# A new issue order for one turn of a block-causal attention with a mixture-of-experts tail, on one Trainium2 core: values copied at once, one PSUM bank fewer

## The chip, the core and the metric

The kernel runs on one core of one Trainium2 chip. The core has five engines that work on their own queues and meet at semaphores: TensorE (PE, matmuls and transposes; PEld is its weight load), VectorE (DVE), ScalarE (ACT), GpSimd (POOL) and SyncE (SP, which here only issues DMAs). The metric is the device time of one execution in microseconds, lower is better. The time of a kernel is the median of several executions; before and after are compared on the same chip.

## What is computed

The reference, cut to what matters (batch 8, 8 heads, 576 positions, 64 per head; 4608 tokens, 8 experts of 512 to 1024 to 512, at most 80 tokens each):

```
scores = (q @ k.T) / sqrt(64);  scores[block_i < block_j] = -1e9     # blocks of 64 positions
attn   = exp(scores - max);  attn /= sum + 1e-9;  x = attn @ v       # per batch and head
logits = x @ w_gate;  e = argmax(logits);  gate = softmax(logits)[e] # x as 4608 x 512
for each expert: of its tokens keep the `capacity` with the largest gate
    out[token] = gate * (relu(x[token] @ w1[e]) @ w2[e]);  every other row is 0
```

## The kernel before, in words

The attention works on **pairs**: two heads of one batch, 32 pairs in all, four to a batch. Head 0 lies on partitions 0 to 63 and head 1 on 64 to 127. A pair's 576 query positions are five row groups: 0 to 3 of 128 rows, and 4 of 64 rows (both heads side by side in one tile).

A pair goes through these steps. The names are the methods of `Pair` and stand in the tables that the change edits:

- `load`, `load_v`: DMAs on SP's queue. `load` issues four DMAs for q and then four for k, into a buffer pair that two pairs share by turns; so the load for pair i+2 has to wait until pair i's tiles have been transposed.
- `prep 0` and `prep 1`: DVE transposes q (0) or k (1) to T0 or T1 (line 405). POOL then scales T0 (line 408).
- `scores g`: PE computes one PSUM tile of scores (pool `ps_s`, two tiles of two banks): "3", "20" (row groups 2 and 0 together), "1", and `scores_4`. Lines 423, 430 and 439.
- `max g`, `max_4`: DVE takes the negated row maximum from PSUM (lines 444 and 448).
- `soft u h`, `soft_4`: ACT computes the exponential from PSUM into SBUF and sums the rows (lines 452 and 457).
- `back x`: PE transposes blocks of the exponentials into a PSUM tile (line 485): "30" and "31" (row group 3, head 0 or 1), "20", "2", "1", each four blocks; "4" four blocks; "44" one block.
- `take back x`: DVE ("v") or ACT ("a"), by the table `TAKE`, copies that tile to PT in SBUF (lines 519 and 517).
- `values 0` and `values 1`: PE multiplies by v into a PSUM tile (line 505): 512 positions, and the last 64. `take values` copies them to xT on ACT (line 517).
- `flip`: DVE turns xT into Y for the store (line 273).

PSUM has eight banks. `ps_s` takes four; the other four belong to the pool `ps_m`, from which every `back` tile, both `values` tiles and the tiles of the deferred steps below are drawn. A new `ps_m` tile is put in a bank whose last tile has been read out in the order of the program; if that reading is not done when PE gets there, PE waits.

The issue order is written out by hand: the table `TURN` is gone through once per turn, and each entry names a pair relative to the turn's own (0 is this turn's pair, -1 the one before, and so on). Each engine gets its instructions in this order, and the schedule is not touched after that. So `scores`, `max` and `soft` of pair i share a turn with `back 4`, `back 44` and `values` of pair i-1.

When a batch's four pairs are through, nine deferred steps are queued, and the three entries `(0, "step")` of each of the next three turns take one each: turn A does `recip` (DVE), `store` (SP) and `logits 0` (PE, ACT, line 290); turn B does `logits 1`, `logits2 0` and `logits2 1` (PE transposes the logits, line 302, DVE multiplies them, line 308); turn C does `gate` (DVE), `turn` (POOL) and `turn2` (PE, line 356, and DVE, line 360). The fourth turn has no deferred step; it is called plain here. A, B and C come up for seven of the eight batches; the last batch's steps follow the loop, and so does the expert part (lines 814 and on), which both versions share.

Of the kernel before, what the change touches and what calls it, by code (L numbers as in the profile page):

```python
# [7 lines left out]
F32 = mybir.dt.float32  # L8
# [10 lines left out]
P = 128  # L19
# [5 lines left out]
CHUNK = 80  # L25


TAKE = {"back": {"30": "v", "31": "a", "1": "a", "2": "a", "20": "v", "4": "v", "44": "v"}, "values": {0: "a", 1: "a"}}

GROUPS = {"3": ((3, 0),), "20": ((2, 0), (0, 384)), "1": ((1, 0),)}  # L30

# [3 lines left out]
    (0, "begin"),  # L35
    (0, "scores", "3"),
    (0, "scores", "20"),
    (-1, "back", "4"),
    (-1, "back", "44"),
    (0, "max", "3"),  # L40
    (-1, "take", "back", "4"),
    (-1, "take", "back", "44"),
    (0, "max", "20"),
    (0, "soft", 3, 0),
    (0, "soft", 3, 1),
    (-1, "values", 0),
    (0, "soft", 0, 0),
    (0, "soft", 0, 1),
    (-1, "values", 1),
    (0, "step"),  # L50
    (1, "prep", 0),
    (0, "soft", 2, 0),
    (0, "soft", 2, 1),
    (0, "scores", "1"),
    (0, "max", "1"),
    (0, "back", "30"),
    (0, "back", "31"),
    (0, "step"),
    (0, "scores_4"),
    (1, "prep", 1),  # L60
    (-1, "take", "values", 0),
    (0, "take", "back", "31"),
    (0, "take", "back", "30"),
    (0, "soft", 1, 0),
    (0, "soft", 1, 1),
    (0, "max_4"),
    (0, "back", "20"),
    (0, "back", "2"),
    (0, "soft_4"),
    (0, "take", "back", "20"),  # L70
    (0, "take", "back", "2"),
    (-1, "take", "values", 1),
    (0, "step"),
    (0, "back", "1"),
    (0, "take", "back", "1"),
    (-2, "flip"),
)


# [1 line left out]
def tile_attn_moe(ctx, tc, q, k, v, w_gate, w1, w2, capacity, out, xs=None, dbg=None):  # L81
# [170 lines left out]
    ps_m = attp.enter_context(tc.tile_pool(name="ps_m", bufs=4, space=PSUM))  # L252

    class Batch:
        def __init__(self, b):
            self.b = b
            self.xT = big.tile([P, NP, S], F32, name="xT")
            self.Y = big.tile([P, S // 32, NP, 32], F32, name="Y")
            self.sums = sm.tile([P, NT, H], F32, name="sums", bufs=2)
            self.sums4 = sm.tile([P, NP], F32, name="sums4", bufs=2)  # L260
            nc.gpsimd.memset(self.sums[BLK:P, NT - 1, :], 1.0)
            self.rs = sm.tile([P, NT, H], F32, name="rs", bufs=2)
# [110 lines left out]
    class Pair:  # L373


        def __init__(self, i):
            self.i = i
            self.b, self.pr = divmod(i, NP)
            self.h0 = 2 * self.pr
            self.out = {}  # L380
            self.T = []

        def load(self):

# [17 lines left out]
        def prep(self, x):  # L402

            t = qk.tile([P, S], F32, name=f"T{x}")
            nc.vector.transpose(t, self.nat[x].rearrange("p g d -> p (g d)"))  # L405
            self.T.append(t)
            if x == 0:
                nc.gpsimd.tensor_scalar(t, t, scalar1=SCALE, scalar2=1.0, op0=ALU.mult, op1=ALU.mult)  # L408

# [51 lines left out]
        def back(self, x):  # L461


            if x == "30":
                self.PT = big.tile([P, 2, 13, P], F32, name="PT")
            PT = self.PT
            row = Pt[self.i % 2]
            pt = ps_m.tile([P, 512], F32, name="pm")
            if x in ("30", "31"):
                h = int(x[1])  # L470
                blocks = [(3, h, j) for j in range(4)]
                dst = PT[:, h, 3:13:3]
            elif x in ("1", "2"):
                u = int(x)
                blocks = [(u, h, j) for h in range(2) for j in range(2)]
                dst = PT[:, :, u:u + 4:3]
            elif x == "20":
                blocks = [b for h in range(2) for b in ((0, h, 0), (2, h, 2))]
                dst = PT[:, :, 0:9:8]
            else:  # L480
                blocks = [(4, None, j) for j in (range(4) if x == "4" else (4,))]
                dst = PT[:, :, 10:12] if x == "4" else PT[:, 0, 7]
            for n_, (u, h, j) in enumerate(blocks):
                src = row[u] if h is None else row[u][:, h]
                nc.tensor.transpose(pt[:, P * n_:P * (n_ + 1)], src[:, P * j:P * (j + 1)], ident)  # L485
            src = pt[:, 0:P * len(blocks)]
            if len(dst.shape) == 3:
                src = src.rearrange("p (j c) -> p j c", c=P)
            elif len(dst.shape) == 4:
                src = src.rearrange("p (h j c) -> p h j c", h=2, c=P)  # L490
            self.out["back", x] = (dst, src)

        def values(self, half):

            av = ps_m.tile([P, 512], F32, name="pm")
            PT = self.PT
            for j in range(4 + half):
                for h in range(2):
                    lhs = self.vt[:, h, :] if j == 4 else self.vn[:, h, j, :]
                    if half == 0:  # L500
                        rhs, c0, end = PT[:, h].rearrange("p b c -> p (b c)")[:, 512 * j:512 + 384 * j], P * j, 512
                    else:
                        b = PT[:, 0, 7] if j == 4 else PT[:, j // 2, 10 + j % 2]
                        rhs, c0, end = b[:, h * BLK:(h + 1) * BLK], 0, BLK
                    nc.tensor.matmul(av[h * D:(h + 1) * D, c0:end], lhsT=lhs, rhs=rhs,  # L505
                                     start=(j == 0), stop=(j == 3 + half))
            self.out["values", half] = ((self.bt.xT[:, self.pr, 0:512], av) if half == 0 else
                                        (self.bt.xT[:, self.pr, 512:S], av[:, 0:BLK]))
# [5 lines left out]
        def take(self, what, x):  # L514

            if TAKE[what][x] == "a":
                nc.scalar.copy(*self.out.pop((what, x)))  # L517
# [71 lines left out]
    ps_m = ctx.enter_context(tc.tile_pool(name="ps_m2", bufs=3, **ps))  # L589
# [292 lines left out]
    with tc.For_i(0, again, 1):  # L882
# [24 lines left out]
        step = 1.0  # L907
# [161 lines left out]
```

## Time and profile before

| | |
|---|---|
| median of 3 runs | 500.9 us (500.85 to 501.71) |
| the profiled execution's own time | 499.57 us |
| its span, from first to last instruction | 497.5 us |
| PE busy with matmuls | 445.1 us, 89% of the span |
| DVE, ACT, POOL busy | 311.7, 253.9, 52.5 us |
| mean granted TensorE clock | 0.976 of full speed |
| attention loop (first scores of the first pair to those of the last) | 7.9 to 347.6 us |

The profile shows one execution. Its time is 2.1 us above its span, and 1.3 us below the median of the runs. A row of the timeline gives the start, the busy time, the engine, the source line and the tiles (out<-in); in square brackets stands how long the engine was idle before and what ended that. Rows of merged instructions carry their count. A matmul's row ends at a modelled time, so PE's pace is best read from the starts of weight loads.

### The profile page before, as it was taken

What the parts mean: (1) busy time and instruction counts of PE and PEld (TensorE: products, weight loads), DVE (VectorE), ACT (ScalarE), POOL (GpSimd) and SP (SyncE); (2) the same over time, 40 slices, a digit from 0 to 9 for tenths busy, and PEclk for the clock granted to TensorE, in tenths of its full rate; (3) what the DMA queues carried; (4) which work ended last, traced back from release to release, by engine and by line L of the source; (5) the groups of instructions that cost most, each with busy time, mean ns of one, the idle gap of its engine ahead of it and who ended that gap; (6) DMA issues with size and microseconds to landing.
All of it is one profiled execution on the core that took longest, in us unless ns stands there. A gap on an engine that the chain in (4) does not pass through costs nothing. (4 is left out here: it accounts for less than half of the span.)

```text
span 497.5 us, 13600 instructions
## 1 busy us (share of the span) xinstructions
PE 445.1 (89%) x5403; PEld 308.3 (62%) x5403; DVE 311.7 (63%) x628; ACT 253.9 (51%) x799; POOL 52.5 (11%) x111
## 2 busy tenths in 40 slices
PE   5999999899899989999998999999985788889991
PEld 3666656556556556655665565556554677778991
DVE  5678787888688878869787886878673220110110
ACT  2677577667666656766765677667612110111100
POOL 1110201010010001001000101010012600000010
PEclk9899999999999999999999999999998599999997
DMA  5776457358647875686679888899596699993010
GB/s 93 134 128 120 79 107 139 67 91 157 104 76 156 176 179 117 126 190 143 129 162 275 180 262 153 177 261 181 132 380 192 190 355 397 398 390 115 17 30 20
DMA packets 232982, 84.32 MB, mean 169 GB/s; under 512 B 196877, under 2 KB 215309, under 8 KB 232912
## 3 DMA queue, kind: packets, MB, share of 16 engines
q1 hardware_dynamic: 231888, 80.93, 66.6%
q0 software_dynamic: 1024, 2.43, 1.7%
q8 instruction: 46, 0.75, 0.7%
q14 instruction: 24, 0.20, 0.1%
HBM read 63.21 MB, written 20.33 MB: 168 GB/s over the span
## 5 line engine op out<-in xcount | busy, mean ns | idle before, releaser
L452 ACT ACTIVATE P<-sc,negm 128x512 f32<-128x512 f32 (+3 forms) x256 | 132.7, 528 | 90.2 <-DVE negm L444 84.2
L444 DVE TENSOR_REDUCE negm<-sc 128x2 f32<-128x1024 f32 (+3 forms) x128 | 101.9, 817 | 46.6 <-PE sc L430 46.4
L485 PE MATMUL pm<-ident,P 128*128 128x128 f32 x800 | 112.8, 281 | 10.6 <-DVE prod L308 5.9
L485 PEld LDWEIGHTS pm<-ident,P 128*128 128x128 f32 x800 | 85.7, 141 | 44.0 <-issue 26.1
L423 PE MATMUL sc<-T,T 64*128 64x128 f32 (+3 forms) x512 | 89.9, 466 | 3.0 <-ACT P L452 1.8
L505 PE MATMUL pm<-PT,vn 128*64 128x64 f32 (+4 forms) x1024 | 91.1, 330 | 0.5 <-DVE PT L519 0.3
L519 DVE COPY PT<-pm 128x512 f32<-128x512 f32 (+1 forms) x128 | 71.0, 575 | 11.1 <-PE pm L485 11.1
L505 PEld LDWEIGHTS pm<-PT,vn 128*64 128x64 f32 x1024 | 52.1, 137 | 40.5 <-issue 34.9
L423 PEld LDWEIGHTS sc<-T,T 64*128 64x128 f32 x512 | 41.6, 186 | 31.4 <-issue 7.1
L517 ACT COPY PT<-pm 128x512 f32<-128x512 f32 x96 | 56.4, 589 | 2.4 <-PE pm L485 0.3
L408 POOL TENSOR_SCALAR T<-T 128x576 f32<-128x576 f32 x32 | 21.5, 671 | 307.0 <-PE pm L505 140.3
L452 ACT ACTIVATION_READ_ACCUMULATOR P<-sc,negm 128x1 f32 x256 | 52.1, 204 | 0.0
L405 DVE STREAM_TRANSPOSE T<-ld 128x576 f32<-128x576 f32 x64 | 48.8, 763 | 3.7 <-DMA ld<-in_k_dram 2.0
L814 PE MATMUL ps<-xsT,w 128*64 128x80 f32 x1024 | 41.6, 242 | 5.4 <-issue 5.4
L814 PEld LDWEIGHTS ps<-xsT,w 128*64 128x64 f32 x1024 | 39.3, 144 | 5.7 <-issue 5.1
L814 PE MATMUL av<-hT,w 128*64 128x80 f32 x1024 | 38.3, 234 | 4.4 <-issue 4.4
L814 PEld LDWEIGHTS av<-hT,w 128*64 128x64 f32 x1024 | 36.5, 137 | 6.3 <-issue 6.3
L439 PE MATMUL sc<-T,T 64*64 64x288 f32 x256 | 39.0, 424 | 0.7 <-ACT P L452 0.7
L457 ACT ACTIVATE P<-sc,negm 128x576 f32<-128x576 f32 x32 | 23.7, 740 | 24.9 <-DVE negm L448 24.9
L834 ACT ACTIVATE hT<-ps 128x320 f32<-128x320 f32 x16 | 7.0, 437 | 50.2 <-PE ps L814 50.2
L842 DVE COPY yT<-av 128x320 f32<-128x320 f32 x8 | 3.9, 492 | 37.2 <-PE av L814 37.2
L448 DVE TENSOR_REDUCE negm<-sc 128x1 f32<-128x576 f32 x32 | 24.0, 751 | 5.0 <-PE sc L439 4.9
(158 smaller groups left out, 304.1 us busy)
## 6 DMA issues: line engine op xcount, KB each, us to landing
w<-in_moe_w_dram SPq DMA_DIRECT2D x16, 2048.0 KB, 16.7
ld<-in_q_dram SPq DMA_DIRECT2D x128, 72.0 KB, 2.7
ld<-in_k_dram SPq DMA_DIRECT2D x128, 72.0 KB, 2.7
xs<-Y SPq DMA_DIRECT2D x32, 288.0 KB, 5.3
out_dram<-zero SPq DMA_DIRECT2D x18, 512.0 KB, 3.5
vn<-in_v_dram SPq DMA_DIRECT2D x64, 128.0 KB, 2.8
vt<-in_v_dram SPq DMA_DIRECT2D x32, 32.0 KB, 2.5
xs<-rs SPq DMA_DIRECT2D x8, 16.0 KB, 4.3
```

The costliest lines, as they stand in the source:

```text
L405: nc.vector.transpose(t, self.nat[x].rearrange("p g d -> p (g d)"))
L423: nc.tensor.matmul(s[:, h, c:c + P * (u + 1)], lhsT=self.T[0][r, P * u:P * (u + 1)], rhs=self.T[1][r, 0:P * (u + 1)], start=(x == 0), stop ...
L439: nc.tensor.matmul(s[r, c, 0:288], lhsT=self.T[0][r, 512:S], rhs=self.T[1][r, 288 * c:288 * (c + 1)], start=True, stop=True)
L444: nc.vector.tensor_reduce(self.negm[:, u], self.s[g][:, :, c:c + P * (u + 1)], axis=AX.X, op=ALU.max, negate=True)
L448: nc.vector.tensor_reduce(self.negm[:, 4, 0:1], self.s["4"][:, :, 0:288], axis=AX.XY, op=ALU.max, negate=True)
L452: nc.scalar.activation(Pt[self.i % 2][u][:, h], self.s[g][:, h, c:c + P * (u + 1)], AF.Exp, bias=self.negm[:, u, h:h + 1], scale=1.0, accu ...
L457: nc.scalar.activation(Pt[self.i % 2][4][:, 0:S].rearrange("p (c k) -> p c k", c=2), self.s["4"][:, :, 0:288], AF.Exp, bias=self.negm[:, 4 ...
L485: nc.tensor.transpose(pt[:, P * n_:P * (n_ + 1)], src[:, P * j:P * (j + 1)], ident)
L505: nc.tensor.matmul(av[h * D:(h + 1) * D, c0:end], lhsT=lhs, rhs=rhs, start=(j == 0), stop=(j == 3 + half))
L517: nc.scalar.copy(*self.out.pop((what, x)))
L519: nc.vector.tensor_copy(*self.out.pop((what, x)))
L814: yield nc.tensor.matmul(dst(b)[64 * c:64 * (c + 1)], lhsT=w_[:, a, col:col + 64], rhs=x_[:, a], start=(a == 0), stop=(a == n - 1))
```

## The change

It edits the table `TURN` and four other lines. On DVE, k is transposed before q, early in the turn, and the copy of `back 20` and that of `back 44` move to ACT. On ACT, both copies of the values stand together behind the exponentials of row groups 3, 2 and 0. `values 1` no longer draws a tile from `ps_m` but uses columns 128 to 191 of the tile of `back 44`. Since k is now transposed first, q and k are kept by name (`self.T[x]`) and not in the order of arrival. The second and third deferred step of a turn stand at other places: behind `scores 1`, and behind `scores_4`.

```
-TAKE = {"back": {... "20": "v", "4": "v", "44": "v"}, ...}
+TAKE = {"back": {... "20": "a", "4": "v", "44": "a"}, ...}
 TURN = (
...
-    (0, "step"),
-    (1, "prep", 0),
+    (-1, "values", 1),
+    (1, "prep", 1),
...
-            self.T = []
+            self.T = {}
...
-            self.T.append(t)
+            self.T[x] = t
...
             self.out["back", x] = (dst, src)
+            if x == "44":
+                self.shared = pt
...
-            av = ps_m.tile([P, 512], F32, name="pm")
+            av = ps_m.tile([P, 512], F32, name="pm") if half == 0 else self.shared[:, P:2 * P]
```

Behind the change the source lines from 493 on stand two lines further down in the changed file (519 is 521 there, 517 is 519).

The order of DVE in one plain turn, before: row maxima (`negm`), copies of "4" (2x256) and "44" (128), T0 from q, T1 from k, copies of "30" and "20", the flip (Y). The number behind a name tells tiles apart.

```order
L444 TENSOR_REDUCE negm_809<-sc_810 128x2
L519 COPY PT_733<-pm_822 128x2x256
L519 COPY PT_733<-pm_827 128x128
L444 TENSOR_REDUCE negm_809<-sc_815 128x2 x2
L405 STREAM_TRANSPOSE T0_858<-ld0_653 128x576
L444 TENSOR_REDUCE negm_809<-sc_863 128x2
L405 STREAM_TRANSPOSE T1_885<-ld1_654 128x576
L519 COPY PT_869<-pm_870 128x4x128
L448 TENSOR_REDUCE negm_809<-sc_880 128x1
L519 COPY PT_869<-pm_893 128x2x2x128
L273 STREAM_TRANSPOSE Y_214<-xT_213 128x18x32
```

The same turn of DVE in the changed kernel:

```order
L444 TENSOR_REDUCE negm_805<-sc_806 128x2
L444 TENSOR_REDUCE negm_805<-sc_811 128x2 x2
L521 COPY PT_732<-pm_821 128x2x256
L405 STREAM_TRANSPOSE T1_853<-ld1_651 128x576
L444 TENSOR_REDUCE negm_805<-sc_859 128x2
L405 STREAM_TRANSPOSE T0_878<-ld0_650 128x576
L521 COPY PT_867<-pm_868 128x4x128
L448 TENSOR_REDUCE negm_805<-sc_882 128x1
L273 STREAM_TRANSPOSE Y_214<-xT_213 128x18x32
```

T1 (k) has moved ahead of the maximum of "1" and T0 (q) behind it; the copies of "44" and "20" are gone from DVE.

The order of ACT in the same turn, before: exponentials (P), then the copy of `values 0` (xT, 512), of "31", and near the end that of `values 1` (xT, 64) between the copies of "2" and "1".

```order
L452 ACTIVATE P1_3_131,sums_670<-sc_810,negm_809 128x512 x2
L452 ACTIVATE P1_0_128,sums_670<-sc_815,negm_809 128x128 x2
L452 ACTIVATE P1_2_130,sums_670<-sc_815,negm_809 128x384 x2
L517 COPY xT_668<-pm_836 128x512
L517 COPY PT_869<-pm_875 128x4x128
L452 ACTIVATE P1_1_129,sums_670<-sc_863,negm_809 128x256 x2
L457 ACTIVATE P1_4_132,sums4_671<-sc_880,negm_809 128x576
L517 COPY PT_869<-pm_898 128x2x2x128
L517 COPY xT_668<-pm_847 128x64
L517 COPY PT_869<-pm_907 128x2x2x128
```

And in the changed kernel:

```order
L519 COPY PT_732<-pm_819 128x128
L452 ACTIVATE P1_3_131,sums_667<-sc_806,negm_805 128x512 x2
L452 ACTIVATE P1_2_130,sums_667<-sc_811,negm_805 128x384 x2
L452 ACTIVATE P1_0_128,sums_667<-sc_811,negm_805 128x128 x2
L519 COPY xT_665<-pm_819 128x64
L519 COPY xT_665<-pm_830 128x512
L452 ACTIVATE P1_1_129,sums_667<-sc_859,negm_805 128x256 x2
L519 COPY PT_867<-pm_873 128x4x128
L457 ACTIVATE P1_4_132,sums4_668<-sc_882,negm_805 128x576
L519 COPY PT_867<-pm_900 128x2x2x128
L519 COPY PT_867<-pm_888 128x2x2x128
L519 COPY PT_867<-pm_893 128x2x2x128
```

The copy of `values 1` has moved from the end of the turn to its middle, and reads the tile (pm_819) that the copy of "44" has read; three copies of transposes now end the turn.

PE's order in a turn B, before, from `logits 1` on: line 302 are the transposes of the logits, line 485 those of the exponentials.

```order
L290 MATMUL pm_1113<-xT_213,wgd_99 32x192 x4
L423 MATMUL sc_1124<-T1_1014,T0_981 128x256 x2
...
L485 MATMUL pm_1131<-ident_79,P1_3_131 128x128 x4
L485 MATMUL pm_1136<-ident_79,P1_3_131 128x128 x4
L302 MATMUL pm_1141<-ident_79,lgT_1036 128x128 x4
L439 MATMUL sc_1148<-T1_1014,T0_981 64x288 x4
...
L485 MATMUL pm_1166<-ident_79,P1_2_130 128x128 x4
L302 MATMUL pm_1175<-ident_79,lgT_1036 64x128
L485 MATMUL pm_1179<-ident_79,P1_1_129 128x128 x4
```

In the changed kernel:

```order
L290 MATMUL pm_1109<-xT_213,wgd_99 32x192 x4
L423 MATMUL sc_1118<-T1_971,T0_1006 128x256 x2
...
L302 MATMUL pm_1124<-ident_79,lgT_1016 128x128 x4
L485 MATMUL pm_1134<-ident_79,P1_3_131 128x128 x4
L485 MATMUL pm_1139<-ident_79,P1_3_131 128x128 x4
L439 MATMUL sc_1148<-T1_971,T0_1006 64x288 x4
L302 MATMUL pm_1154<-ident_79,lgT_1016 64x128
...
L485 MATMUL pm_1163<-ident_79,P1_2_130 128x128 x4
L485 MATMUL pm_1170<-ident_79,P1_1_129 128x128 x4
```

Both groups of line 302 have moved up by one place; apart from the deferred steps, PE's order in a turn differs only in that "44" stands ahead of "4".

## Rows read from the trace of the kernel before

**Rows 1.** The page, busy time of the engines and share of the span.

```profile
PE 445.1 (89%) x5403; PEld 308.3 (62%) x5403; DVE 311.7 (63%) x628; ACT 253.9 (51%) x799; POOL 52.5 (11%) x111
```

**Rows 2.** Busy time by turn (windows): turns A, B, C and a plain one.

```profile
core 0: us, PE busy (x) PEld busy (x) DVE busy (x) ACT busy (x) POOL busy (x), PEclk, DMA share, GB/s
202.75:213.62 10.87, 10.87 (x101) 6.56 (x100) 9.46 (x18) 8.20 (x28) 0.67 (x1) 1.00 0.72 145
213.62:226.22 12.60, 11.36 (x105) 7.05 (x105) 8.31 (x14) 7.67 (x25) 0.77 (x2) 1.00 0.85 184
226.22:237.42 11.20, 10.41 (x109) 6.63 (x108) 10.30 (x24) 7.45 (x26) 1.43 (x2) 1.00 0.63 136
237.42:247.36 9.94, 9.94 (x93) 6.42 (x92) 7.37 (x13) 6.61 (x22) 0.67 (x1) 1.00 0.56 129
```

**Rows 3.** Timeline of turn B, from `logits2 0` to the turn's end.

```profile
221.23 0.59 ACT L517 COPY xT<-pm 128x512 f32<-128x512 f32 x1
...
221.87 0.42 PEld L302 LDWEIGHTS pm<-ident,lgT 128*128 128x128 f32 x4 [0.60 <-ACT xT L517]
...
224.40 0.11 PEld L302 LDWEIGHTS pm<-ident,lgT 128*64 128x64 f32 x1
225.44 0.20 DVE L308 TENSOR_TENSOR prod<-pm,rs 64x64 f32<-64x64 f32 x1
225.63 0.42 PEld L485 LDWEIGHTS pm<-ident,P 128*128 128x128 f32 x4 [1.12 <-issue]
226.15 0.22 ACT L517 COPY xT<-pm 128x64 f32<-128x64 f32 x1
```

**Rows 4.** Timeline of turn C, `turn2` and the transposes behind it.

```profile
235.72 0.23 PEld L356 LDWEIGHTS pm<-sp,sameR 128*32 128x32 f32 x16 [0.17 <-issue]
...
236.86 0.63 PE L485 MATMUL pm<-ident,P 128*128 128x128 f32 x4 [0.79 <-DVE Wt L360]
```

**Rows 5.** Groups by line and form, ACT: its copies from PSUM.

```profile
L517 ACT COPY PT<-pm 128x512 f32<-128x512 f32 x96 | 56.4, 589 | 2.4 <-PE pm L485 0.3
...
L517 ACT COPY xT<-pm 128x64 f32<-128x64 f32 x32 | 7.1, 223 | 0.0
```

**Rows 6.** Timeline of DVE in the plain turn from 237.42.

```profile
238.62 1.22 DVE L444 TENSOR_REDUCE negm<-sc 128x2 f32<-128x1024 f32 x1 [1.12 <-PE sc L430]
...
241.01 1.28 DVE L444 TENSOR_REDUCE negm<-sc 128x2 f32<-128x768 f32 x2
242.21 0.77 DVE L405 STREAM_TRANSPOSE T<-ld 128x576 f32<-128x576 f32 x1
243.87 0.69 DVE L444 TENSOR_REDUCE negm<-sc 128x2 f32<-128x512 f32 x1 [0.89 <-PE sc L430]
244.47 0.77 DVE L405 STREAM_TRANSPOSE T<-ld 128x576 f32<-128x576 f32 x1
```

**Rows 7.** Timeline of the start, up to the first scores.

```profile
5.66 0.68 POOL L408 TENSOR_SCALAR T<-T 128x576 f32<-128x576 f32 x1 [3.83 <-DVE T L405]
...
7.00 0.78 DVE L405 STREAM_TRANSPOSE T<-ld 128x576 f32<-128x576 f32 x1 [1.43 <-DMA ld<-in_k_dram]
7.92 1.13 PE L423 MATMUL sc<-T,T 64*128 64x512 f32 x4 [1.11 <-DVE T L405]
```

**Rows 8.** Windows, the first turn (columns as in rows 2).

```profile
8.00:18.00 10.00, 8.21 (x52) 5.17 (x54) 6.60 (x9) 5.95 (x20) 0.67 (x1) 0.83 0.79 136
```

**Rows 9.** Timeline of SP's queue, the loads for pairs 24 and 31.

```profile
243.00 3.83 SPq L391 DMA_DIRECT2D ld<-in_q_dram  x4
...
327.83 8.62 SPq L391 DMA_DIRECT2D ld<-in_q_dram  x4
336.55 2.72 SPq L391 DMA_DIRECT2D ld<-in_k_dram  x4
```

**Rows 10.** The page, DMA issues: KB each, us from issue to landing.

```profile
ld<-in_k_dram SPq DMA_DIRECT2D x128, 72.0 KB, 2.7
```

**Rows 11.** Timeline, k of the last pair transposed, and that pair's first scores.

```profile
343.81 0.77 DVE L405 STREAM_TRANSPOSE T<-ld 128x576 f32<-128x576 f32 x1
...
347.62 1.13 PE L423 MATMUL sc<-T,T 64*128 64x512 f32 x4
```

More of the change, by code (lines that the diff above doesn't have):

```diff
@@ L25 @@
 CHUNK = 80
-TAKE = {"back": {"30": "v", "31": "a", "1": "a", "2": "a", "20": "v", "4": "v", "44": "v"}, "values": {0: "a", 1: "a"}}
+TAKE = {"back": {"30": "v", "31": "a", "1": "a", "2": "a", "20": "a", "4": "v", "44": "a"}, "values": {0: "a", 1: "a"}}
 GROUPS = {"3": ((3, 0),), "20": ((2, 0), (0, 384)), "1": ((1, 0),)}
@@ L37 @@
     (0, "scores", "20"),
+    (0, "max", "3"),
+    (-1, "back", "44"),
     (-1, "back", "4"),
-    (-1, "back", "44"),
-    (0, "max", "3"),
-    (-1, "take", "back", "4"),
     (-1, "take", "back", "44"),
     (0, "max", "20"),
+    (-1, "take", "back", "4"),
+    (-1, "values", 0),
+    (0, "soft", 3, 1),
     (0, "soft", 3, 0),
[L45 to L49, printed above, removed]
-    (0, "step"),
-    (1, "prep", 0),
     (0, "soft", 2, 0),
     (0, "soft", 2, 1),
+    (-1, "values", 1),
+    (1, "prep", 1),
+    (0, "soft", 0, 1),
+    (0, "step"),
+    (0, "soft", 0, 0),
+    (-1, "take", "values", 1),
+    (-1, "take", "values", 0),
     (0, "scores", "1"),
     (0, "max", "1"),
+    (0, "step"),
+    (0, "soft", 1, 0),
+    (0, "soft", 1, 1),
     (0, "back", "30"),
     (0, "back", "31"),
+    (1, "prep", 0),
+    (0, "take", "back", "30"),
+    (0, "scores_4"),
+    (0, "max_4"),
     (0, "step"),
[L59 to L66, printed above, removed]
     (0, "back", "20"),
     (0, "back", "2"),
+    (0, "take", "back", "31"),
+    (-2, "flip"),
+    (0, "back", "1"),
     (0, "soft_4"),
+    (0, "take", "back", "1"),
     (0, "take", "back", "20"),
     (0, "take", "back", "2"),
[L72 to L76, printed above, removed]
 )
```

## The prediction, made before the changed kernel ran

> **What bounds the kernel now.** I read the page first, then the windows by turn, then the timelines of the turns that are too long, then those of the queues that feed the loop. In the page's busy times [rows 1] PE leads with 445.1 us, 89% of the span; DVE has 63% and ACT 51%. That is an average over turns of different kinds, so the windows by turn come next [rows 2]. A plain turn lasts 9.94 us and PE is busy for 9.94 of them, DVE for 7.37, ACT for 6.61: PE alone sets it. Turn A takes 10.87, again with no idle PE; its 0.93 over a plain turn is the matmuls of `logits 0`. Turn B takes 12.60 with PE busy 11.36, so 1.24 of it is idle PE; turn C 11.20 with 10.41, so 0.79 is idle. The clock is 1.00 in all of them. What can be won without taking matmuls away is therefore in B and C, and the timelines say where. In B [rows 3] the weight load of `logits2 0` (line 302) waited 0.60 us for ACT's copy of `values 0`, which ran from 221.23 to 221.82; and `back 1` started at 225.63, 1.12 us behind the end of the load of `logits2 1` at 224.51. The view writes "issue" there, but DVE's line 308, which reads the first tile of line 302 out of PSUM, ended at 225.64: `back 1` was given that tile's bank. In C [rows 4] `back 1` waited 0.79 us for DVE's copy to Wt, which reads the tile of `turn2`. All three are waits for one of the four banks of `ps_m`. One of the four is held by `values 1` for half a turn: in the row of its copy in B [rows 3] it is emptied at 226.15 to 226.37, in the turn's last instant, though PE has long written it.
>
> **The change part by part.** *The bank.* `values 1` now lives in the tile of `back 44`, so the turn draws one tile fewer from `ps_m`, and both copies of the values run in the middle of the turn. The tile that `logits2`, `turn2` and `back 1` are given is then one that was emptied earlier, and lines 308 and 360 have the time of a whole further tile before somebody needs theirs. I take the three waits as gone: 0.60 + 1.12 + 0.79 = 2.51 us a batch. The lower bound is the idle time that the windows show, 1.24 + 0.79 = 2.03 (PE's busy time counts some of the first wait). Nothing is late next in these turns as far as the rows go: behind the waits PE has only work that is as far along as in a plain turn. In A nothing waits, and I put it at nothing. A batch has one turn of each, and seven batches have them.
>
> *What the sharing costs.* `values 1` must not write before ACT has copied "44". ACT does that first thing in its turn; a 128x512 copy takes 589 ns and a 128x64 one 223 ns [rows 5], so this one of 128x128 lies between them, nearer the small one: 0.28. Between "44" and `values 1` PE has the four transposes of "4" and `values 0` to do, together about 2 us by my count of the turn, so the copy is over long before and costs nothing. If it ever came late, each us would cost one us in each of 31 turns; that is among the rivals.
>
> The Trainium skill says in Perfetto Trace Analysis, section "Matmuls", that independent groups of matmuls should rotate through different PSUM banks, so that emptying one overlaps the next group; two groups in one bank, as here, go against it. By it PE would stand for the copy, and the sum below would come out as in the second rival. That the copy is over before PE is back at that bank speaks against it here.
>
> *The two copies that go to ACT.* DVE loses "20" (589 ns as ACT's price, taken for both) and "44"; ACT goes from 6.61 to 6.61 + 0.59 + 0.28 = 7.5 of 9.94 us. In a plain turn neither engine is the bound, so this gives nothing and costs nothing, as long as ACT's copies keep ahead of PE: 2.4 us of spare time cover them. If one of the three copies that now end the turn comes late for `values 0` of the next, PE waits by as much; from 0 to 0.28 us a turn, and I take 0.
>
> *The start.* Before the loop, k is transposed second because its data lands second: DVE starts on it at 7.00 having waited for the load, and the first scores start at 7.92 [rows 7]. POOL's scaling of T0, 0.68 us at 5.66, lies under that wait. With k first, DVE waits for it with q already there, transposes k until 7.78, then q (0.78), then POOL scales (0.68), and then come the scores with the 0.14 that lay between k's end and theirs: 9.38 instead of 7.92. I take 1.4 lost, with 0.78 + 0.68 = 1.46 as the upper bound and 0.7 as the lower (if only the POOL part counted). The first turn has a lower clock, 0.83 over its window [rows 8], which is between the levels of 1.2 and 2.4 GHz; the 10 us at 0.83 hold 1.7 us of full-speed time, so a shift of that stretch could move the sum by up to 1.7 either way. I take 0.
>
> *The loads.* The load for pair i+2 writes the buffer that pair i's transposes read, four q DMAs first. In the plain turn from 237.42, q is transposed from 242.21 to 242.98 [rows 6], and the next q load is issued at 243.00 [rows 9]: it waited for that. In the new order q stands behind the maximum of "1", where k stood, at 244.47: 2.26 later in the turn, call it 2.3. That matters only if the queue is a bound. From 243.00 to 327.83 SP issues the loads of seven pairs, 84.83 / 7 = 12.1 us for each [rows 9], weights and stores between them, while the turns last (10.87 + 12.60 + 11.20 + 9.94) / 4 = 11.15 on average. So late in the loop the queue is slower than the turns, and lives on its lead. Its last k load is issued from 336.55 to 339.27, with the last of its four DMAs some 0.68 before that, and takes 2.7 us to land [rows 10], so at about 341.3 to 341.5; DVE transposes that k at 343.81 and the scores follow at 347.62 [rows 11], 6.1 us behind the landing. There the lead is 2.3 us.
>
> In the new kernel the queue runs the same instructions from the same kind of start. Four batches are through by turn 21, so that turn starts 4 x 2.51 - 1.4 = 8.6 us earlier; the queue's last stretch starts 8.6 - 2.3 = 6.3 earlier, and the last k lands at about 341.5 - 6.3 = 335.2. From there to the scores the new order needs k (0.77), the maximum of "1" (0.69), q (0.77) [rows 6], POOL (0.68) and PE's transposes that stand ahead of the scores, in all about 4.6 us (the parts named make 2.9; the rest, an estimate, is copies on DVE and PE's queue). The scores start at 339.8 instead of 347.62. The gain that reaches the end is 7.8 us, not the 7 x 2.51 - 1.4 = 16.2 that the banks alone would give: the rest is taken up by the wait for k and q in the last three batches, at line 405. Behind the loop nothing is changed.
>
> **The rivals.** *The queue does not limit.* If SP's 12.1 us for each pair is itself a matter of waiting for the turns (its DMAs queue behind each other, and the DMA share in [rows 2] is 0.56 to 0.85, not 1), then all seven batches give: 16.2, or 483.4 for the profiled execution. For it: the share below 1. Against it: issues of 8.62 us for four q DMAs [rows 9], which is a queue that is full.
>
> *ACT's copies come late.* With 7.5 of 9.94 us and three copies at the turn's end, `values 0` or the tile of "44" waits for ACT a little in every turn. At 0.1 to 0.15 us in 31 turns that takes 3 to 4.7 us of the 7.8: 496 to 498; with the whole copy of 0.28 in each it would take all of it. Against it: 2.4 us of spare time per turn.
>
> *Slower.* The waits for banks stay, since `back 1` is still given the bank of a late tile, and what is left is the start and the loads: k first costs 1.4, the queue's start 2.3, less 6.1 - 4.6 = 1.5 that the shorter way from landing to scores gives back: 2.2 lost, 501.8 profiled, 503.1 as a median. It decides from the point at which the banks give back less than 2.2 / 4 = 0.55 us a batch of the 2.51. For it: the new order also moves the steps. Against it: one tile fewer for the same four banks.
>
> *Plain turns shorten too.* PE is busy 9.94 of 9.94 but its weight loads only 6.42 [rows 2]; were DVE (7.37 plus what it waits for) in truth what paces the turn, taking 0.8 us of copies from it would give some 0.4 us a turn, 8 more by turn 21: near 484. Against it: PE shows no idle time in plain turns, and its order is kept but for "44" and "4". The Trainium skill, Perfetto Trace Analysis, section "Identifying the Most-Contended Engine", holds that matmul busy time is a bad metric and the weight loads' share a good one; by that, PE with 65% has headroom and this rival is the forecast.
>
> *Nothing to see.* If the queue gives back only what the loads lose, 0 to 2 us; 0.2% of 500.9 is 1.0 us, about what a measurement of this kernel can tell from no change.
>
> **How the numbers follow.** The profiled execution took 499.57 us, 2.1 over its span and 1.3 under the median of 500.9. It becomes 499.57 - 7.8 = 491.8; at the median 493.1. Chances: the forecast 0.60 (491 to 496 by its own bounds: 2.03 in place of 2.51 takes 1.9, the start's bound adds 0.7); the queue does not limit 0.16 (484.7 as a median); ACT late 0.11; plain turns shorter 0.04; slower 0.06; nothing to see 0.03. Range 484 to 497: it takes in the queue without a limit and the copies that come late, and leaves out slower and nothing, and the tails. Faster by over 0.2%: 0.60 + 0.16 + 0.11 + 0.04 = 0.91; within 0.2%: 0.03; slower: 0.06.
>
> **What the profile of the changed kernel would show.** Windows by turn: plain turns still 9.94, B near 12.60 - 1.72 = 10.9 and C near 11.20 - 0.79 = 10.4, with no idle PE. In the chain of waits no line 485 behind Wt or line 308. The first scores at about 9.3. SP without a gap in the last quarter, and in some of the turns from 24 on PE's scores waiting for line 405 and that for ld<-in_q or in_k. The forecast is wrong if B and C keep their idle time (the bank was not the reason), if plain turns grow (ACT), or if the late turns show no wait for loads (then it is 484).

## The result and the profile after

The changed kernel takes 488.89 us (median of 4 runs, 488.18 to 489.11) beside 500.88 (4 runs) of the kernel before; the ratio is 0.9762 [0.9735, 0.9789]. The forecast was 493.1 in a range of 484 to 497. The profiled execution has a span of 486.92 us instead of 497.49, which is 10.57 less where the forecast had 7.8.

On the page, PE's busy time is what it was [rows 1], in a span that is 10.6 us shorter; DVE has given 28 us away and ACT has taken 18.5.

```profile
PE 445.3 (91%) x5403; PEld 310.5 (64%) x5403; DVE 283.4 (58%) x564; ACT 272.4 (56%) x863; POOL 52.8 (11%) x111
```

The windows of the same four turns, A, B, C and plain (columns as in rows 2):

```profile
196.57:207.29 10.72, 10.72 (x101) 6.57 (x100) 8.00 (x15) 8.11 (x27) 0.67 (x1) 1.00 0.76 150
207.29:218.20 10.91, 10.91 (x105) 7.08 (x104) 7.37 (x12) 8.39 (x27) 0.77 (x2) 1.00 0.78 160
218.20:228.42 10.22, 10.22 (x108) 6.64 (x108) 9.52 (x22) 8.15 (x28) 1.47 (x2) 1.00 0.78 179
228.42:238.36 9.94, 9.94 (x93) 6.41 (x92) 7.00 (x10) 7.64 (x24) 0.67 (x1) 1.00 0.80 175
```

PE is busy in each turn from end to end. The plain turn has kept its 9.94; A is 0.15 shorter than in [rows 2], B 1.69 and C 0.98: 2.82 us a batch (2.81 by the starts of the turns) where the forecast took 2.51. In the timeline of B and C the waits of [rows 3, 4] are gone:

```profile
214.08 0.42 PEld L302 LDWEIGHTS pm<-ident,lgT 128*128 128x128 f32 x4 [0.24 <-issue]
...
214.80 0.41 DVE L308 TENSOR_TENSOR prod<-pm,rs 128x256 f32<-128x256 f32 x1
...
216.66 0.11 PEld L302 LDWEIGHTS pm<-ident,lgT 128*64 128x64 f32 x1 [0.44 <-ACT PT L519]
216.69 1.34 PEld L485 LDWEIGHTS pm<-ident,P 128*128 128x128 f32 x12
...
217.45 0.21 DVE L308 TENSOR_TENSOR prod<-pm,rs 64x64 f32<-64x64 f32 x1
...
226.68 0.23 PEld L356 LDWEIGHTS pm<-sp,sameR 128*32 128x32 f32 x16 [0.44 <-issue]
...
226.96 1.29 PEld L485 LDWEIGHTS pm<-ident,P 128*128 128x128 f32 x12
...
227.47 0.21 DVE L360 COPY Wt<-pm 128x40 f32<-128x40 f32 x1
```

The reader is to see that twelve weight loads of line 485 run on behind line 302 and behind line 356 without a break, while DVE reads the steps' tiles during them: no row of these turns waits for line 308 or 360 any more.

The start goes as the forecast had it, with k transposed first, then q, then POOL's scaling of q, and the first scores at 9.22 (9.3 to 9.4 forecast, 7.92 before [rows 7]):

```profile
6.96 1.44 DVE L405 STREAM_TRANSPOSE T<-ld 128x576 f32<-128x576 f32 x2 [3.75 <-DMA ld<-in_k_dram]
...
9.22 2.08 PE L423 MATMUL sc<-T,T 64*128 64x512 f32 x4 [2.17 <-POOL T L408]
```

And one of the late turns, the C from 301.78, waits for a load. Its window, then DVE's and PE's rows in it:

```profile
301.78:316.34 14.56, 11.65 (x108) 7.25 (x107) 9.51 (x22) 8.25 (x28) 1.46 (x2) 0.88 0.86 178
```

```profile
310.36 0.78 DVE L405 STREAM_TRANSPOSE T<-ld 128x576 f32<-128x576 f32 x1 [4.37 <-DMA ld<-in_k_dram]
...
312.11 0.29 PEld L439 LDWEIGHTS sc<-T,T 64*64 64x64 f32 x4 [3.15 <-ACT P L452]
```

DVE stands 4.37 us at line 405 for pair 29's k; the maximum of "1" is queued behind it on DVE, the exponentials behind that on ACT, and PE's `scores_4` needs their PSUM tile. The turn loses 4.35 us to a C without a wait: 2.9 as idle PE and 1.4 because PE's work behind the wait ran at a lower clock (0.88 over the window, busy 11.65 instead of 10.22). Cut at the clock's changes, the window shows it: PE is all but idle for 3.25 us, and then the granted clock is 0.50, the lower of its two levels (1.2 of 2.4 GHz), for 3.42 us.

```profile
308.50:311.75 3.25, 0.70 (x7) 0.47 (x5) 1.32 (x5) 0.27 (x2) 0.00 (x0) 1.00 0.82 208
311.75:315.17 3.42, 3.05 (x27) 1.61 (x28) 3.28 (x10) 2.40 (x9) 1.46 (x2) 0.50 0.97 184
```

In SP's queue the reason stands two turns earlier, from 280.29 on: a weight load (w), the q and k loads behind it, a store of four DMAs and more, and only then the loads of pair 29.

```profile
236.27 1.96 SPq L391 DMA_DIRECT2D ld<-in_q_dram  x4
...
280.29 0.61 SPq L235 DMA_DIRECT2D w<-in_moe_w_dram  x1
281.00 6.57 SPq L391 DMA_DIRECT2D ld<-in_q_dram  x4
287.61 5.07 SPq L391 DMA_DIRECT2D ld<-in_k_dram  x4
...
294.60 4.08 SPq L278 DMA_DIRECT2D xs<-Y  x4
...
305.63 2.12 SPq L391 DMA_DIRECT2D ld<-in_k_dram  x4
...
317.77 0.61 SPq L235 DMA_DIRECT2D w<-in_moe_w_dram  x1
318.48 9.08 SPq L391 DMA_DIRECT2D ld<-in_q_dram  x4
327.60 2.51 SPq L391 DMA_DIRECT2D ld<-in_k_dram  x4
```

The last k is transposed at 332.30, after a wait, and the last first scores start at 336.99 instead of 347.62 [rows 11]:

```profile
332.30 0.78 DVE L405 STREAM_TRANSPOSE T<-ld 128x576 f32<-128x576 f32 x1 [1.81 <-DMA ld<-in_k_dram]
...
336.99 1.13 PE L423 MATMUL sc<-T,T 64*128 64x512 f32 x4
```

From the starts of the turns the 10.57 us add up: start -1.30, first turn -1.26 (11.06 instead of 9.80), turn 5 +0.32, six batches of 2.81 +16.86, the wait of turn 28 -4.35, and +0.30 in turns 27, 30 and the tail.

### The profile page after: what moved, and what is told of

It reads as the page before. It is cut to its first block, busy times and chain, and to the rows that moved or that the text cites. A ratio compares the mean times of both kernels' runs of the same rounds, so it can differ in the third digit from the quotient of the medians.

```text
span 486.9 us, 13564 instructions
## 1 busy us (share of the span) xinstructions
PE 445.3 (91%) x5403; PEld 310.5 (64%) x5403; DVE 283.4 (58%) x564; ACT 272.4 (56%) x863; POOL 52.8 (11%) x111
## 3 DMA queue, kind: packets, MB, share of 16 engines
q0 software_dynamic: 1024, 2.43, 1.7%
## 5 line engine op out<-in xcount | busy, mean ns | idle before, releaser
L444 DVE TENSOR_REDUCE negm<-sc 128x2 f32<-128x1024 f32 (+3 forms) x128 | 99.6, 819 | 74.2 <-PE sc L430 74.1
L485 PE MATMUL pm<-ident,P 128*128 128x128 f32 x800 | 108.9, 280 | 0.3 <-ACT P L457 0.2
L485 PEld LDWEIGHTS pm<-ident,P 128*128 128x128 f32 x800 | 87.3, 141 | 21.8 <-issue 15.2
L423 PE MATMUL sc<-T,T 64*128 64x128 f32 (+3 forms) x512 | 92.3, 476 | 3.0 <-POOL T L408 2.2
L519 ACT COPY PT<-pm 128x512 f32<-128x512 f32 (+1 forms) x160 | 77.0, 529 | 23.4 <-PE pm L485 22.9
L452 ACT ACTIVATION_READ_ACCUMULATOR P<-sc,negm 128x1 f32 x256 | 54.3, 212 | 0.0
L521 DVE COPY PT<-pm 128x512 f32<-128x512 f32 x64 | 42.7, 667 | 0.6 <-PE pm L485 0.5
```

Of the source, the lines that this page charges most:

```text
L423: nc.tensor.matmul(s[:, h, c:c + P * (u + 1)], lhsT=self.T[0][r, P * u:P * (u + 1)], rhs=self.T[1][r, 0:P * (u + 1)], start=(x == 0), stop ...
L444: nc.vector.tensor_reduce(self.negm[:, u], self.s[g][:, :, c:c + P * (u + 1)], axis=AX.X, op=ALU.max, negate=True)
L452: nc.scalar.activation(Pt[self.i % 2][u][:, h], self.s[g][:, h, c:c + P * (u + 1)], AF.Exp, bias=self.negm[:, u, h:h + 1], scale=1.0, accu ...
L521: nc.vector.tensor_copy(*self.out.pop((what, x)))
```

## The experiments

Theory 1, the prediction's: one tile fewer from `ps_m` frees the banks. Theory 2: the sharing is nothing, the copies of the values come earlier, and that frees them. A third, that the new places of the deferred steps do it too, came up after the eighth run. The queue has its own four runs. A kernel before ran beside each group: 498.09 us in the first (E1 to E4), 498.55 in the second (E5 to E8), 498.32 in the third (E9 to E12), where the run of the result had 500.88; so runs of different groups are compared by their ratios and by the starts of their turns. The changed kernel itself ran only beside the 500.88. E2, whose turns are the same up to the wait for loads, gave a ratio of 0.9808 beside 498.09, so the whole change is worth some 1.9 to 2.4%.

**E1, the sharing alone,** in the kernel before.

```
+            if x == "44":
+                self.shared = pt
...
+            av = ps_m.tile([P, 512], F32, name="pm") if half == 0 else self.shared[:, P:2 * P]
```

> The kernel before, with one thing of the change: values 1 uses columns 128 to 191 of the tile of back 44 and draws none from ps_m; every copy stays where it was. Theory 1 (the prediction's paragraph on the bank: one tile fewer is what frees the banks): most of the three waits of 2.51 us a batch go, turn B comes near 10.9 and C near 10.4, six batches before the last first scores, so 486 to 491 us. Theory 2 (what counts is when the copies of the values empty their banks, and this kernel copies as late as before): B stays 12.6, C 11.2, 500.9 us within 0.2%.

497.46 us, ratio 0.9991 [0.9971, 1.0011]. Windows of its B and C:

```profile
214.49:227.09 12.60, 11.35 (x105) 7.04 (x105) 8.30 (x14) 7.67 (x25) 0.77 (x2) 1.00 0.86 186
227.09:238.29 11.20, 10.41 (x109) 6.62 (x108) 10.30 (x24) 7.46 (x26) 1.43 (x2) 1.00 0.57 126
```

The same turns as in [rows 2], to 0.01 us. Theory 1 falls.

**E2, all but the sharing:** the changed kernel, in which `values 1` draws its own tile.

```
-            av = ps_m.tile([P, 512], F32, name="pm") if half == 0 else self.shared[:, P:2 * P]
+            av = ps_m.tile([P, 512], F32, name="pm")
```

> The changed kernel without the sharing: values 1 draws its own tile from ps_m again; order and copies as in the changed kernel. Theory 1 (the shared bank): the waits of B and C come back, up to 2.8 us a batch, 17 us in six batches of which the loads hide some: 500 to 504 us. Theory 2 (the time of the copies): the turns stay at 10.72, 10.92, 10.22 and 9.94, 488.9 us within 0.2%.

487.48 us, 0.9808 [0.9762, 0.9854], not to be told from the changed kernel. B and C:

```profile
205.98:216.89 10.91, 10.91 (x105) 7.08 (x104) 7.37 (x12) 8.39 (x27) 0.77 (x2) 1.00 0.74 149
216.89:227.11 10.22, 10.22 (x108) 6.65 (x108) 9.51 (x22) 8.15 (x28) 1.46 (x2) 1.00 0.81 183
```

Without the sharing the waits for banks stay away: in these turns it neither gives nor costs anything. The wait for loads is not quite the same, 13.32 us in turn 28 and 11.54 in turn 30.

**E3, one copy alone:** the kernel before, with the copy of `values 1` behind that of `values 0`.

```
     (-1, "take", "values", 0),
+    (-1, "take", "values", 1),
     (0, "take", "back", "31"),
...
     (0, "take", "back", "2"),
-    (-1, "take", "values", 1),
```

> The kernel before, with one other thing of the change: the copy of values 1 stands directly behind that of values 0 on ACT (it stood between the copies of 2 and 1 at the turn's end). No sharing, q first, the steps where they were. Theory 1: no tile is saved, so 500.9 us. Theory 2: the bank of values 1 is free some 4 us earlier, so back 1 finds a bank; the 1.12 of B and the 0.79 of C go, the 0.60 behind the copy of values 0 stays: B near 11.5, C near 10.4, 1.9 us a batch, six batches, 11.4 us at the last first scores, with nothing lost at the start: 489 to 491 us.

486.30 us, 0.9759 [0.9729, 0.9789]: one line moved gives as much as the whole change. B and C:

```profile
208.08:219.61 11.53, 11.16 (x106) 7.09 (x105) 7.26 (x12) 6.59 (x23) 0.77 (x2) 1.00 0.84 188
219.61:229.98 10.37, 10.37 (x109) 6.62 (x108) 10.12 (x24) 7.36 (x25) 1.43 (x2) 1.00 0.63 139
```

The bank of `values 1`, emptied late, was what `back 1` lacked: 1.07 of B and 0.83 of C went, as expected. The 0.60 us that line 302 waits for the copy of `values 0` is still there (weight load at 216.33). It gives 1.9 us a batch where the whole change gives 2.8, but it loses nothing at the start, and turn 30 waits 1.07 us for loads (11.94).

**E4, q first:** the changed kernel with `prep` 0 and 1 exchanged.

```
-    (1, "prep", 1),
+    (1, "prep", 0),
     (0, "soft", 0, 1),
...
-    (1, "prep", 0),
+    (1, "prep", 1),
     (0, "take", "back", "30"),
```

> The changed kernel with prep 0 and prep 1 exchanged in the table: q is transposed early in a turn, k later, as in the kernel before; all else as in the changed kernel. Theory on the start: the first scores come back from 9.22 to 7.92, and what the first turn lost in clock (1.26) with them: 2.5 us. Theory on the queue (it bounds the last quarter): SP's stretch starts 2.3 us earlier in its turn and 2.5 earlier with the start, so the wait of 4.37 us in turn 28 for k of pair 29 goes for the most part: in all 5 to 7 us, 482 to 484 us. Rival (the queue's end is set by its DMAs, not by its start): the wait moves to a later pair and only the start's 2.5 are won, 486.4 us.

483.67 us, 0.9710 [0.9680, 0.9741]. The first scores start at 8.15. Turn 28 takes 11.91 instead of 14.57, but turn 30 is now 12.55, with a wait for the last q:

```profile
299.45:311.36 11.91, 10.57 (x108) 6.62 (x107) 9.61 (x22) 7.81 (x27) 1.46 (x2) 1.00 0.81 183
321.30:333.85 12.55, 10.93 (x100) 6.54 (x99) 8.08 (x15) 8.02 (x27) 0.88 (x2) 1.00 0.82 203
```

Both theories have a part: the start comes back, most of the wait of turn 28 goes, and some of it returns at the end of SP's queue. That is less than the 5 to 7 us expected: by the ratios 2.6 us beside the changed kernel (3.8 beside E2 of the same group), by the last first scores 3.1 (333.85 instead of 336.99). Of these 3.1 the first turn gives 1.26 (9.80 instead of 11.06), which is not the order's doing, as the part on the start below shows; the start gives 1.07, turns 28 and 30 together 0.8.

**E5, E6, E7, SP's other work earlier,** in the changed kernel (E5), in the one before (E6), and with q first (E7).

```
-            clear(i - n + (nz if ov is not None else 0))
+            clear(i - 8)
...
-            if i in range(n - 3 * FW0, n, 3):
+            if i in range(6, 6 + 4 * FW0, 4):
```

> The changed kernel with SP's other work done earlier: the three weight loads of the loop in turns 6, 10 and 14 instead of 23, 26 and 29, and the 18 stores of zeros in turns 8 to 25 instead of 14 to 31. Theory (SP's queue bounds the last quarter): the loads of q and k behind the weights no longer take 5.5 to 9.1 and 2.5 to 5.1 us for four DMAs but some 2.7 and 2.1; the wait of 4.37 us in turn 28 for k of pair 29 goes, and no other wait for a load comes, so the last first scores start at 332.6 and the time falls by 4.4: 484 to 485 us. Rival (the wait is the store of xs ahead of that load, some 7 us of issuing, and not the weights): turn 28 keeps its wait and the time stays at 488.9.

487.59 us, 0.9791 [0.9745, 0.9838], and neither answer was right: from turn 17 on no turn waits for a load, and turn 28 is 10.22, but turn 16 takes 16.26. Its window, DVE's row and SP's queue ahead of it:

```profile
176.66:192.92 16.26, 11.86 (x108) 7.67 (x107) 9.51 (x22) 8.26 (x28) 1.46 (x2) 0.90 0.81 169
```

```profile
186.68 0.78 DVE L405 STREAM_TRANSPOSE T<-ld 128x576 f32<-128x576 f32 x1 [5.80 <-DMA ld<-in_k_dram]
```

```profile
155.71 0.61 SPq L235 DMA_DIRECT2D w<-in_moe_w_dram  x1
156.41 9.51 SPq L391 DMA_DIRECT2D ld<-in_q_dram  x4
...
170.99 4.15 SPq L278 DMA_DIRECT2D xs<-Y  x4
...
179.06 2.73 SPq L391 DMA_DIRECT2D ld<-in_q_dram  x4
```

A weight load and a batch's store, one behind the other, stand ahead of this wait as they do ahead of that in turn 28 of the changed kernel. So it is not the last quarter as such. The pair alone is not enough either: the weight loads of turns 6 and 10 have a store behind them too, and turns 8 and 12 keep their 10.22. That the queue's lead was used up by the third pair is the likely reading; no run tests it alone.

> The same lightening of SP's queue in the kernel before. Theory: its turns wait for no load worth naming (1.6 and 2.0 us of DVE's idle time in three places, and 0.2 us of turn 27), so the time stays within 0.2% of 498 to 501 us. Rival (the queue was a bound before too): some us faster.

498.14 us, 1.0002 [0.9985, 1.0020]: the kernel before had lead enough, the queue cost it nothing.

> The changed kernel with q first and the lighter queue together. Theory: turns 28 and 30 lose their 1.7 and 1.84 us of waiting for loads, so 3.5 us less than with q first alone: 480 us, with turns of 10.72, 10.92, 10.22 and 9.94 to the end. Rival: the wait is only moved, 483 us.

479.65 us, 0.9615 [0.9589, 0.9642], the fastest of all, with no turn made longer by a wait; the last first scores start at 330.60, 6.4 us ahead of the changed kernel's (4.35 from turn 28, 1.08 from the start, 0.97 from the first turn). Its turn 28:

```profile
299.73:309.94 10.21, 10.21 (x108) 6.64 (x107) 9.72 (x22) 7.91 (x27) 1.47 (x2) 1.00 0.61 107
```

The same weight load in turn 14 makes no wait here: with q first the load for the next pair but one starts earlier in the turn, and that lead is enough.

**E8, the late copy** in the changed kernel.

```
-    (-1, "take", "values", 1),
     (-1, "take", "values", 0),
...
     (0, "soft_4"),
+    (-1, "take", "values", 1),
```

> The changed kernel, with only the copy of values 1 put back to the turn's end, behind the exponential of row group 4 (the tile of 44 is then held that long); values 0 is copied in the middle as in the changed kernel. Theory 2 in its plain form (the early copy of values 1 is what removes the waits): B and C come back to some 12.0 and 11.0, 4 to 5 us slower than the changed kernel without its wait of turn 28, 489 to 493 us. Rival (the new order has further slack: the steps stand where a bank is free anyway, and values 0's early copy alone is enough): B and C stay within 0.2 of 10.92 and 10.22, and the time within 1 us of 488.9.

489.71 us, 0.9828 [0.9806, 0.9850]. B takes 11.01 and C 10.22: the rival is right, and theory 2 by itself doesn't explain the changed kernel. Only A grew, to 11.00, where a transpose waits for the copy of `logits 0` instead. Turn 28 waits for loads as before (14.80).

```profile
207.58:218.59 11.01, 11.01 (x105) 7.06 (x105) 7.47 (x12) 8.13 (x27) 0.77 (x2) 1.00 0.75 153
218.59:228.81 10.22, 10.22 (x109) 6.64 (x108) 9.42 (x22) 8.04 (x29) 1.47 (x2) 1.00 0.80 187
```

```profile
206.50 0.91 PEld L485 LDWEIGHTS pm<-ident,P 128*128 128x128 f32 x8 [0.25 <-ACT lgT L292]
```

**E9, both back:** E8 with the steps where the kernel before has them.

```
     (-1, "values", 1),
+    (0, "step"),
     (1, "prep", 1),
...
     (0, "back", "31"),
+    (0, "step"),
...
+    (0, "step"),
     (0, "back", "1"),
```

(The three steps of the changed order are taken out.)

> The changed kernel with two things put back: the deferred steps stand where they stood in the kernel before (behind values 1, behind back 31, ahead of back 1), and the copy of values 1 is at the turn's end. Sharing, k first, TAKE and the rest of the order stay. Theory 3 (two causes, each enough alone: the values' banks are empty early, or the steps draw their tiles at places where another bank is empty): with both taken back the waits return, B above 12 and C near 10.8, and with the late tile of 44 A above 11: some 4 us a batch slower than the changed kernel, with no wait for loads any more, 498 to 503 us. Rival (something else of the new order, as the copies that end the turn, holds the banks free): B and C stay under 11.1 and 10.4, 488 to 491 us.

502.54 us, 1.0079 [1.0040, 1.0118]: the rest of the change, sharing and all, is slower than the kernel before. A, B and C together take 34.6 us, as in [rows 2] (34.67): the banks give nothing back. A has a wait that the kernel before has not, 1.29 us at `back 1` for the copy of `logits 0` (at 215.01). What makes the run slower is the start (9.23 instead of 7.92) and a wait for loads in turn 30 (14.80 us instead of 11.54), which the expectation had ruled out. Turns A, B and C, and the waits at `back 1` in B and C:

```profile
204.06:215.60 11.54, 10.94 (x101) 6.55 (x100) 7.97 (x15) 8.39 (x29) 0.67 (x1) 1.00 0.83 162
215.60:227.89 12.29, 11.32 (x105) 7.04 (x104) 8.13 (x13) 8.26 (x28) 0.77 (x2) 1.00 0.81 179
227.89:238.68 10.79, 10.44 (x109) 6.62 (x108) 8.87 (x21) 8.04 (x26) 1.47 (x2) 1.00 0.64 140
```

```profile
227.31 0.42 PEld L485 LDWEIGHTS pm<-ident,P 128*128 128x128 f32 x4 [1.24 <-DVE prod L308]
...
238.09 0.42 PEld L485 LDWEIGHTS pm<-ident,P 128*128 128x128 f32 x4 [0.47 <-DVE Wt L360]
```

**E10, the steps alone,** in the kernel before.

```
     (0, "max", "1"),
+    (0, "step"),
     (0, "back", "30"),
     (0, "back", "31"),
-    (0, "step"),
...
     (0, "max_4"),
+    (0, "step"),
...
-    (0, "step"),
     (0, "back", "1"),
```

> The kernel before with only the second and third deferred step moved, to the places that they have in the changed kernel (ahead of back 30, and behind max_4). Copies, sharing, q first as before. Theory 3: the moved steps alone take most of the waits: B near 11.7, C near 10.6, A 10.72: 1.6 us a batch, six batches, about 9 to 10 us at the last first scores: 488 to 491 us. Rival (the moved steps only shift PE's waits, since the banks of the values are as late as before): B 12.6, C 11.2, 498 us.

489.08 us, 0.9815 [0.9785, 0.9845]. A, B and C:

```profile
198.29:209.00 10.71, 10.71 (x100) 6.57 (x99) 8.93 (x18) 8.05 (x27) 0.67 (x1) 1.00 0.75 151
209.00:220.67 11.67, 11.30 (x106) 7.05 (x105) 8.44 (x14) 7.46 (x25) 0.77 (x2) 1.00 0.74 170
220.67:231.47 10.80, 10.29 (x109) 6.64 (x108) 10.26 (x25) 7.48 (x26) 1.43 (x2) 1.00 0.78 161
```

That is 1.5 us a batch. Each of the two steps has moved ahead of two tiles, "30" and "31" or "20" and "2". No `back 1` waits for a step's tile; what is left in B is the wait for the copy of `values 0`, 0.60 us, now at `back 31` (217.26), and in C `turn2` waits for POOL, which it now follows sooner.

**E11, the steps back** in the changed kernel, copies early (the steps as in E9, the copies as in the changed kernel).

> The changed kernel with the deferred steps where they stood in the kernel before; the copies of the values early as in the changed kernel. Theory 3: the early copies alone keep the waits away: B 10.9, C near 10.4, A 10.87, so 0.3 us a batch slower than the changed kernel by turn 21, which the wait for loads of pairs 29 and 31 takes up: within 1 us of the changed kernel, 487 to 489 us. Rival: the steps' places carry the gain, B near 12 and C near 11, 494 us or more.

490.30 us, 0.9834 [0.9801, 0.9868]. A 10.87, B and C:

```profile
208.72:219.66 10.94, 10.94 (x105) 7.11 (x104) 6.97 (x11) 8.17 (x28) 0.77 (x2) 1.00 0.76 154
219.66:230.03 10.37, 10.37 (x109) 6.62 (x108) 9.91 (x23) 8.58 (x28) 1.47 (x2) 1.00 0.80 186
```

The turns are as expected; the time is 1.3 us above the expected bound. Its turns 28, 29 and 30 take 13.48, 10.84 and 11.85, so loads are waited for in three places. Theory 3 stands: of the 2.8 us a batch the steps' places alone give 1.5 in the kernel before (E10) and the early copy alone 1.9 (E3); the changed kernel keeps 2.4 without the early copy (E8) and 2.5 without the new places (E11), and without both it has none (E9). What takes the 0.60 us behind the copy of `values 0` in E11, where the step stands as in E3, was not tested by itself.

**E12, the copies on DVE again** ("20" and "44"), in the changed kernel.

```
-TAKE = {"back": {... "20": "a", "4": "v", "44": "a"}, ...}
+TAKE = {"back": {... "20": "v", "4": "v", "44": "v"}, ...}
```

> The changed kernel with TAKE as in the kernel before: DVE copies the tiles of 20 and 44 again. The prediction: neither engine is the bound of a plain turn, so the plain turns stay at 9.94 and B and C within 0.1 us; the time within 0.3% of the changed kernel's 487 to 489 us. Rival (DVE paces the turn): plain turns some 0.4 us longer, 12 us in all.

488.40 us, 0.9809 [0.9784, 0.9833]. The plain turn takes 9.93, B 10.92 and C 10.22: which engine copies doesn't matter to the turns. Turn 28 takes 16.23 here; with k first and the queue as it was, the changed turns have 13.32 (E2) to 16.23 us there, and most of that spread is the clock (last section).

## Why the prediction held, point by point

- **Where the time could be won** held. Plain turns kept 9.94, and idle PE in B and C was what went. The rule of the Trainium skill (Perfetto Trace Analysis, section "Identifying the Most-Contended Engine") would have had headroom in PE, with weight loads at 65% of the turn; two DVE copies more or less (E12) moved no plain turn, so here the measurement decides for PE's busy time. With it fell the rival that plain turns shorten, and the one that ACT's copies come late (its upper price, 498, lay outside the range that was said to hold it).
- **The bank** held in size (2.81 us a batch for 2.51; A's 0.15 had been put at nothing, and B and C gave all of their waits), and not in its cause. The paragraph put the sharing first and the time of the copies beside it. The sharing does nothing (E1, E2). Two other parts do it, and in the changed kernel either keeps most of the gain: the early copies of the values (E3, E11), or the places of the steps (E10, E8). The prediction gave the steps' places no price. That 2.51 came out so near is therefore in part luck. A reading went astray here: the row of line 308 at 225.44 in [rows 3] (64x64) reads the tile of `logits2 1`, not the first tile of line 302. So in B, as in C, `back 1` had been given the bank of the step straight ahead of it, and with that step moved (E10) no `back 1` waits for such a tile. The prediction also took seven batches into the sum without the queue; by the last first scores only six have had their B and C.
- **What the sharing costs**: nothing, as forecast. The Trainium skill's rule on rotating banks (Perfetto Trace Analysis, section "Matmuls") cost nothing where it was broken (E1: 0.9991). The copy of "44" was over before PE came back: in E1's plain turn from 238.29 it ends at 241.96, and `values 1` first writes at 243.28.
- **The start** held for its mechanism: 1.30 for 1.4. The other 1.26, of the first turn, lie within the 1.7 that the prediction named for its clock and put at 0. They are not the new order's: with k first E2 and E8 take 9.84 and 9.80 us for that turn, as the kernel before does (9.80), and with q first E1 takes 10.76. The last section says what the clock does there.
- **The loads** held in place and kind, and failed in size. Of the 4.2 us by which the forecast was too slow, 2.7 are in the profiled execution, and this step makes them; the other 1.5 are the 1.3 that was added from the profiled execution to the median, where the changed kernel's median lies 0.2 below its profiled execution (489.11). The prediction took 16.2 down to 7.8 by moving the queue's last stretch unchanged. SP started it 6.73 us earlier (6.3 forecast), but it was also 2.43 shorter: 93.84 us from 236.27 to 330.11 instead of 96.27 from 243.00 to 339.27, of which the first four q DMAs alone are 1.87 (1.96 for 3.83). From the last k's landing to the scores it took 4.7 us (4.6 forecast). The wait that lengthened a turn came in turn 28 alone and not in three batches.
- **The rival on the slower side** is real: E9 is that mechanism, banks that give nothing back with the start and the loads lost, and its ratio of 1.0079 [1.0040, 1.0118] lies beside the 503.1 / 500.9 = 1.0044 that it was given. What kept the changed kernel from it are two parts of the change, each of which would have saved most of the gain (E8, E11).
- **The loads' rival** ("does not limit", 483.4 profiled, 484.7 as a median) fell for the changed kernel. No turn waits for loads in E7 (479.65 us), where q is first and the weights are early; the start's 1.3 is not lost there either.

## What to carry to other kernels

When tiles rotate through few banks, ask for each tile when it is read out and who draws its bank next: moving one copy forward (E3), or one consumer to a place where an empty bank comes up, takes most of the wait away, and saving a tile need not. Undo each part alone and all together before you credit one, since two parts can hide behind each other. A reordering that frees a loop's inner engine also eats the lead of the queue that feeds it: put the release of a load's buffer (here, q's transposition) as early as it goes (E4), and then move large loads to where the queue still has lead (E7; by itself, in E5, that only moved the wait).

## What the runs showed that I had not expected

- Directly behind a weight load of 2 MB the issue of four q DMAs takes 5.49, 6.57 and 9.08 us on SP in the changed kernel, and 9.51 in E5, where 2.7 is usual; the store behind it then adds some 7. In E5's turn 6, where 4.6 us lay between the two, it took 2.75.
- A wait can cost more than its length: in turn 28 PE was idle for 2.9 us, and the clock over the window was 0.88, which took another 1.4; in E12 it was 3.5 us of idle PE, 0.79 and another 2.5. In E2 PE was idle for nearly as long (2.8 us), and the clock stayed 1.00.
- The first score matmuls took 2.08 us instead of 1.13 in 7 of 14 profiled executions, behind idle times of 0.78 to 2.54 us and with no relation to them. In the changed kernel the window view gives a clock of 1.00 there, but the trace's own clock records begin only at 18.2 us, and the view counts time without a record as 1.00. The weight loads of line 485 take 226 ns each ahead of 18.2 us and 140 behind it; in the kernel before they take 224 where the granted clock is 0.5. So that stretch ran at the lower level. In all seven runs with 2.08 us the records begin behind the first scores, at 11.6 to 18.9 us, and in the other seven ahead of them, at 6.4 to 7.7. What decides when the clock rises stays open; over the 14 runs the first turn takes 8.36 to 11.39 us.
